# A new order for weight tiles and lead-in in a kernel of retention and two MLPs

## The chip, the cores and the metric

The kernel runs on one core of a Trainium2 chip. The metric is the device time of one execution in microseconds (us). TensorE multiplies matrices, VectorE and ScalarE do elementwise work, GpSimd a little, and SyncE (SP) issues all DMAs from one queue, in order. Each engine works through its own queue in program order and waits on semaphores.

## The reference, cut to what matters

Eight heads of linear attention with a decaying state, then an MLP with a squared ReLU, then RMS norm and a gated MLP. All is float32.

```python
for t in range(S):                                    # B, H, S, D = 4, 8, 768, 64
    state = gamma * state + k[:, :, t] (x) v[:, :, t]  # outer product, per head
    y[:, :, t] = scale * (q[:, :, t] @ state)
x = y as (3072, 512)
h = np.maximum(x @ w_in, 0.0)                         # 512 -> 2048
x = h * h @ w_out                                     # 2048 -> 512
xn = x / sqrt(mean(x * x) + 1e-6) * rms_g
g = xn @ w_gate                                       # 512 -> 1536
out = (g / (1 + exp(-g)) * (xn @ w_val)) @ w_out2
```

## The kernel before, in words

**Retention.** The sequence is cut into 24 chunks of 128 tokens, numbered so that four in a row are the same part of the four batches. For a chunk, `decay_q` and `decay_v` (lines 475 to 490) scale q and v by powers of the decay; `scores` (500) multiplies k and q on TensorE and masks the product on VectorE (line 512); `values` (527) multiplies masked scores and v, and, from chunk 4 on, the old state (`st_in`) and q; `take_x` (546) splits the result into a high part (ScalarE, line 77) and a low part (VectorE, line 74); `into_state` (517) makes the product of k and v, and `take_state` (550) adds it to the state and scales it on ScalarE. `show_state` (492) copies a state to where TensorE reads it.

**Float32 by three products.** TensorE multiplies rounded operands. Each operand is held as high and low part, and `mm3` (151) issues three matmuls: high by high (line 152), high by low (153), low by high (154).

**Weight tiles.** The weights arrive as raw 64-bit words and are put together in steps, one per 128x512 tile, by `tick` (133). In step i, `magnitude` (115) makes the absolute value of tile i+1 from its raw words on ScalarE; `finish1` (91) takes tile i-1, makes its high part on ScalarE (line 94) and hands back a function for the low part on VectorE; `convert` (120) puts tile i together in three VectorE instructions (123 to 127) and fetches tile i+3; the low part comes last. Three buffers `f` hold the tiles in work, and three hold raw words. The first 32 steps are the first MLP's tiles, in and out weight in turn; 36 more are for the second MLP's, which `finish2` (97) writes to DRAM.

**First MLP.** `block1` (635) runs over 16 steps f for each of six blocks of 512 tokens: a projection (`proj`, 12 matmuls), the squared ReLU on ScalarE (`act1`, lines 179 to 182), the low part of s on VectorE, and the output product (`out1`, 12 matmuls) of the step before. `early1` and `late1` (673 to 679) put a weight step ahead of the projection and after it. One retention chunk of the next block is done in each four steps f: scores after the projection of f = 0, 4, 8, 12; state and values one f later; scaling of v and the state copy at f = 2 and of q at f = 3, for the chunk to come. So VectorE's queue has a chunk's q behind the weight steps of that f.

**Lead-in.** Lines 561 to 618 load chunks 0 to 3 and the first weights, run retention for these four, and run the first two weight steps among them. TensorE's sums are in eight banks: `acc` has four, `h` two, `sc` and `xs` one each. A bank is free for the next product when its readers are done. The state products of the four chunks use `sc` and `xs` in turn (line 617).

The order of the work is written out by hand: each engine's queue has the instructions in the order of the program text. The last two thirds of the kernel (second MLP) are not touched.

Of the kernel before, what the change touches and what calls it, by code (L numbers as in the profile page):

```python
# [26 lines left out]
CB = TB // C  # L27
# [18 lines left out]
def retention_then_two_mlps(  # L46
    ctx: ExitStack, tc: tile.TileContext, qT, kT, kn, vn, w1i, w1o, w2g, w2v, w2o, rmsg, tri, qdec, vdec, sdec, out
):
    nc = tc.nc
# [14 lines left out]
    def bank(tag, shape, name, bufs):  # L64
        return ps.tile(shape, F32, tag=tag, name=name, bufs=bufs)
# [10 lines left out]
    def split(dst_h, dst_l, src, el):  # L76
        nc.scalar.copy(dst_h, src)  # L77
        low(el, dst_l, src, dst_h)
# [28 lines left out]
    loads, sizes, done = {}, {}, {}  # L107
    at = [0]
# [6 lines left out]
    def magnitude(i):  # L115
        if i < len(steps):
            sizes[i] = cf.tile([128, 512], F32, tag="f", name="f")
            nc.scalar.activation(sizes[i], loads[i].bitcast(F32)[:, :, 1], AF.Abs, scale=REBIAS)

    def convert(i):  # L120
        raw, f = loads.pop(i), sizes.pop(i)
        m = f.bitcast(I32)
        nc.vector.tensor_scalar(m, m, 3, None, op0=ALU.logical_shift_left)
        nc.vector.scalar_tensor_tensor(
            out=m, in0=raw[:, :, 0], scalar=29, in1=m, op0=ALU.logical_shift_right, op1=ALU.bitwise_or
        )
        nc.vector.scalar_tensor_tensor(
            out=m, in0=raw[:, :, 1], scalar=-(1 << 31), in1=m, op0=ALU.bitwise_and, op1=ALU.bitwise_or
        )
        done[i] = f  # L130
        fetch(i + 3)

    def tick():

        i = at[0]
        if i > len(steps):
            return
        if i == 0:
            magnitude(0)
        magnitude(i + 1)  # L140
        rest_of = None
        if i:
            fn, key, _ = steps[i - 1]
            rest_of = fn(key, done.pop(i - 1))
        if i < len(steps):
            convert(i)
        if rest_of is not None:
            rest_of()
        at[0] = i + 1

# [272 lines left out]
    with tc.manual_schedule():  # L423
        nc.vector.memset(ones, 1.0)

        with ExitStack() as rctx:
# [48 lines left out]
            def decay_q(c, eng):  # L475
                if c < NCH:
                    eng.tensor_tensor(out=chunk[c][0], in0=chunk[c][0], in1=qdec_sb, op=ALU.mult)

            def decay_v(c, eng):

                if c >= NCH:
                    return
                vv = chunk[c][2].rearrange("p a h d -> p (a h) d")
                if eng is nc.scalar:
                    for h in range(H):
                        nc.scalar.activation(vv[:, h, :], vv[:, h, :], AF.Copy, scale=vdec_sb[:, h:h + 1])
                else:
                    eng.tensor_tensor(
                        out=vv, in0=vv, in1=vdec_sb.unsqueeze(2).to_broadcast([128, H, D]), op=ALU.mult
                    )  # L490

            def show_state(c):
                if B <= c < NCH:
                    for b in heads:
                        nc.scalar.copy(st_in[b, :, b], st[c % B][b])
# [4 lines left out]
            def scores(c, tags, early=False):  # L500

                qq, k_, _, _ = chunk[c]
                sc = [bank(*tag) for tag in tags]
                if early:
                    P = wp.tile([128, 2, 512], F32, tag="w", name="Pt").rearrange("p h (a i) -> p h a i", a=NP)
                else:
                    P = rp.tile([128, 2, NP, C], F32, tag="P", name="Pt", bufs=1)
                for p in range(NP):
                    for h, b in enumerate(heads):
                        nc.tensor.matmul(sc[h][:, p, :], k_[b, p, :], qq[b, p, :], start=True, stop=True)  # L510
                for h in range(2):
                    nc.vector.tensor_tensor(
                        out=P[:, h], in0=sc[h], in1=tri_sb.unsqueeze(1).to_broadcast([128, NP, C]), op=ALU.mult
                    )
                pt[c] = P

            def into_state(c, tag, bufs):
                if c // B == CPB - 1:
                    return None
                _, _, vv, kk = chunk[c]  # L520
                kv = bank(tag, [128, NP, D], "kv", bufs)
                for p in range(NP):
                    for h, b in enumerate(heads):
                        nc.tensor.matmul(kv[b, p, :], kk[:, p, h, :], vv[:, p, h, :], start=True, stop=True)
                return kv

            def values(c, tag, bufs):
                P = pt.pop(c)
                qq, _, vv, _ = chunk[c]
                xs = bank(tag, [128, NP, C], "xs", bufs)  # L530

                for p in range(NP):
                    for h, b in enumerate(heads):
                        nc.tensor.matmul(
                            xs[b, p, :], vv[:, p, h, :], P[:, h, p, :], start=(p == 0),
                            stop=(c < B and p == NP - 1), skip_group_check=True,
                        )
                if c >= B:
                    for p in range(NP):
                        nc.tensor.matmul(  # L540
                            xs[:, p, :], st_in[:, p, :], qq[:, p, :], start=False, stop=(p == NP - 1),
                            skip_group_check=True,
                        )
                return xs

            def take_x(c, x, xs):
                o = slice((c % B) * C, (c % B + 1) * C)
                split(x[0][:, :, o], x[1][:, :, o], xs, nc.vector)

            def take_state(c, kv):  # L550
                n = c % B
                if kv is None:
                    return
                if c >= B:
                    nc.vector.tensor_tensor(out=st[n], in0=st[n], in1=kv, op=ALU.add)
                for p in range(NP):
                    nc.scalar.activation(
                        st[n][:, p, :], (st[n] if c >= B else kv)[:, p, :], AF.Copy, scale=sdec_sb[:, p:p + 1]
                    )
# [30 lines left out]

            def decay0(c):
                decay_q(c, nc.vector)
                decay_v(c, nc.scalar)

            decay0(0)
            decay0(1)
            scores(0, early_banks, early=True)
            keep_warm(WARM // 2)
            scores(1, early_banks, early=True)
            decay0(2)  # L600
            xs = values(0, "xs", 1)
            scores(2, early_banks, early=True)
            take_x(0, cur, xs)
            decay0(3)
            xs = values(1, "sc", 1)
            scores(3, early_banks, early=True)
            take_x(1, cur, xs)
            tick()
            xs = values(2, "h", 2)
            take_x(2, cur, xs)  # L610
            tick()
            xs = values(3, "xs", 1)
            take_x(3, cur, xs)
            decay_q(CB, nc.vector)
            decay_v(CB, nc.scalar)
            for c in range(CB):
                take_state(c, into_state(c, "xs" if c % 2 else "sc", 1))
            show_state(CB)

            prev = None  # L620
# [14 lines left out]
            def block1(j, x, ret, early, late):  # L635
                nonlocal prev, at_chunk
                acc = []
                for f in range(NF1):
# [3 lines left out]
                    while ("i", f) not in W:  # L642
                        tick()
# [29 lines left out]
            def early1(f):  # L673
                if at[0] <= n1_steps or f % 2 == 0 or f // 2 < per_block - NF1 // 2:
                    tick()

            def late1(f):
                if at[0] <= n1_steps:
                    tick()

            for j in range(NB - 1):
                nxt = new_x()
                block1(j, cur, nxt, early1, late1)
                cur = nxt
# [11 lines left out]
        xs = prep_x(0, lambda: [quarter[0, h].rearrange("p m n -> p (m n)") for h in range(2)])  # L696
# [48 lines left out]
        for s in range(NS):  # L745
            acc = []
# [14 lines left out]
            xs = iter(())  # L761
            if s + 1 < NS:
                xs = prep_x(
                    2 * (s + 1), lambda: [tp.tile([128, TB], F32, tag="sq", name="yl") for _ in range(2)], lazy=s == 0
                )
# [82 lines left out]
```

## Time and profile before

| | us |
|---|---|
| median of 3 runs | 1208.14 (1207.37 to 1209.44) |
| profiled execution, its own time | 1207.8 |
| its span, first to last instruction | 1206.0 |
| TensorE busy with matmuls | 1174.0 |
| VectorE busy | 706.3 |
| ScalarE busy | 571.4 |

The profile is of one execution. TensorE is shown busy 97% of the span; its matmuls overlap, and their ends are modelled. The first of 40 slices of the span is at six tenths, the next at eight, the rest at nine or more but for the last.

### The profile page before, as it was taken

The page shows a single profiled execution, that of the slowest core. Times are in us where ns is not written, and L with a number is a line of the kernel's source. Part 1 is how long each engine was busy: PE and PEld are TensorE (multiplying, and loading weights), DVE is VectorE, ACT ScalarE, POOL GpSimd, SP SyncE. Part 2 cuts the span into 40 slices and gives each one's busy share as a digit, 9 for nine tenths or more (in the row PEclk, how much of TensorE's full clock was granted, in tenths as well). Part 3 has the DMA queues.
Part 4 walks back from the last instruction along what each step waited for, and adds up shares of the span by engine and source line. Part 5 has one row for each costly group of instructions (what it writes and reads, how often), then busy time and mean ns, then how long its engine had stood idle before and what let it go on. Part 6 is the DMA issues. An engine that isn't in the chain of part 4 may idle for free.

```text
span 1206.0 us, 15522 instructions
## 1 busy us (share of the span) xinstructions
PE 1174.0 (97%) x6006; PEld 952.4 (79%) x6006; DVE 706.3 (59%) x1097; ACT 571.4 (47%) x1084; POOL 95.5 (8%) x76
## 2 busy tenths in 40 slices
PE   6899999999999999999999999999999999999998
PEld 5677788888888887887777788888788888788887
DVE  5788854254344326431654677776677776677740
ACT  6767644444444444333554544544544444444431
POOL 0000031140022104002002000000000000000000
PEclk9999999999999999999999899999999999999999
DMA  8455543442334435311223111133111132111001
GB/s 300 154 186 176 200 140 108 129 149 88 114 116 141 123 94 151 94 36 59 82 79 114 36 36 44 36 105 110 39 35 44 36 123 81 51 35 44 27 1 70
DMA packets 56042, 114.08 MB, mean 95 GB/s; under 512 B 6280, under 2 KB 12576, under 8 KB 55968
## 3 DMA queue, kind: packets, MB, share of 16 engines
q1 hardware_dynamic: 55968, 113.09, 29.7%
q8 instruction: 47, 0.77, 0.3%
q14 instruction: 27, 0.22, 0.1%
HBM read 91.04 MB, written 22.03 MB: 94 GB/s over the span
## 4 chain that ended last, share of the span: by engine, by line
PE 85%; DVE 5%; ACT 5%; issue 2%; DMA 2%; SPq 0%; DVEq 0%; ACTq 0%
PE h L154 7%; PE h L152 6%; PE h L153 6%; PE acc L152 6%; PE acc L153 6%; PE acc L154 6%; PE a L152 5%; PE a L154 5%; PE a L153 5%; PE b L154 4%; PE b L153 4%; PE b L152 4%; PE late L152 3%; PE late L153 3%; PE late L154 3%; PE oacc L154 3%
## 5 line engine op out<-in xcount | busy, mean ns | idle before, releaser
L74 DVE TENSOR_TENSOR s<-r,s 128x512 fp32r<-128x512 f32 x96 | 69.7, 726 | 201.7 <-ACT s L182 201.7
L179 ACT ACTIVATE r<-h 128x512 f32<-128x512 f32 x96 | 57.3, 597 | 224.0 <-PE h L154 224.0
L152 PE MATMUL h<-xh,w_i 128*128 128x512 f32 x384 | 151.9, 395 | 5.6 <-ACT w_i L94 5.6
L152 PE MATMUL acc<-s,w_o 128*128 128x512 f32 x384 | 153.5, 400 | 1.2 <-DVE y L71 1.2
L154 PE MATMUL h<-xh,w_i 128*128 128x512 f32 x384 | 151.6, 395 | 2.1 <-DVE w_i L74 2.1
L153 PE MATMUL acc<-s,w_o 128*128 128x512 f32 x384 | 150.1, 391 | 1.8 <-DVE s L74 1.8
L153 PE MATMUL h<-xl,w_i 128*128 128x512 f32 x384 | 150.3, 391 | 0.0
L154 PE MATMUL acc<-s,w_o 128*128 128x512 f32 x384 | 149.9, 390 | 0.0
L152 PE MATMUL a<-xop,ring 128*128 128x512 f32 x288 | 113.9, 395 | 0.4 <-DVE t L351 0.4
L154 PE MATMUL a<-xop,ring 128*128 128x512 f32 x288 | 112.2, 389 | 0.0
L153 PE MATMUL a<-xop,ring 128*128 128x512 f32 x288 | 112.2, 389 | 0.0
L152 PEld LDWEIGHTS h<-xh,w_i 128*128 128x128 f32 x384 | 72.8, 189 | 24.1 <-ACT w_i L94 8.7
L74 DVE TENSOR_TENSOR ring<-q,ring 128x512 fp32r<-128x512 f32 x90 | 58.8, 686 | 53.3 <-ACT ring L77 53.3
L154 PEld LDWEIGHTS h<-xh,w_i 128*128 128x128 f32 x384 | 72.6, 189 | 21.8 <-DVE w_i L74 6.8
L152 PEld LDWEIGHTS acc<-s,w_o 128*128 128x128 f32 x384 | 72.2, 188 | 17.7 <-DVE y L71 1.6
L153 PEld LDWEIGHTS acc<-s,w_o 128*128 128x128 f32 x384 | 72.2, 188 | 16.8 <-DVE s L74 2.9
L152 PE MATMUL b<-xop,ring 128*128 128x512 f32 x216 | 84.3, 390 | 0.2
L154 PEld LDWEIGHTS acc<-s,w_o 128*128 128x128 f32 x384 | 72.1, 188 | 15.3
L153 PEld LDWEIGHTS h<-xl,w_i 128*128 128x128 f32 x384 | 72.5, 189 | 14.8
L153 PE MATMUL b<-xop,ring 128*128 128x512 f32 x216 | 84.1, 389 | 0.0
L154 PE MATMUL b<-xop,ring 128*128 128x512 f32 x216 | 84.1, 389 | 0.0
L152 PEld LDWEIGHTS a<-xop,ring 128*128 128x128 f32 x288 | 54.2, 188 | 15.5 <-DVE t L351 4.6
(150 smaller groups left out, 2165.1 us busy)
## 6 DMA issues: line engine op xcount, KB each, us to landing
q<-wq SPq DMA_DIRECT2D x72, 256.0 KB, 3.2
raw<-w1i SPq DMA_DIRECT2D x16, 512.0 KB, 3.6
raw<-w1o SPq DMA_DIRECT2D x16, 512.0 KB, 3.6
raw<-w2g SPq DMA_DIRECT2D x12, 512.0 KB, 3.8
raw<-w2v SPq DMA_DIRECT2D x12, 512.0 KB, 3.5
raw<-w2o SPq DMA_DIRECT2D x12, 512.0 KB, 3.9
wq<-f SPq DMA_DIRECT2D x24, 256.0 KB, 3.9
ys<-y SPq DMA_DIRECT2D x24, 256.0 KB, 2.5
```

The lines of the kernel that those rows point to most:

```text
L74: eng.tensor_tensor(out=dst_l, in0=src, in1=dst_h.bitcast(F32), op=ALU.subtract)
L152: nc.tensor.matmul(acc, ah, bh, start=start, stop=False, **more)
L153: nc.tensor.matmul(acc, ah, bl, start=False, stop=False, **more)
L154: nc.tensor.matmul(acc, al, bh, start=False, stop=stop, **more)
L179: nc.scalar.activation(r, h, AF.Relu)
```

## The change

In `tick`, the high part of tile i-1 (`fn`) is issued ahead of the magnitude of tile i+1; with `low_first` the low part is issued ahead of the conversion. In the lead-in, VectorE scales v of chunks 0 to 3 in one instruction each (line 489) where ScalarE did in eight; the first weight step moves ahead of `take_x(1)`, the second behind the state products; values of chunk 3 go to an `h` bank, the four state products to the four `acc` banks, all issued ahead of the second weight step. In the first block an additional step runs where the count of steps reaches 5 and 10, that is at f = 1 and f = 3; the number of steps in all is the same.

```diff
-    def tick():
+    def tick(low_first=False):
...
-        magnitude(i + 1)
-        rest_of = None
+        rest_of = lambda: None
         if i:
             fn, key, _ = steps[i - 1]
-            rest_of = fn(key, done.pop(i - 1))
+            rest_of = fn(key, done.pop(i - 1)) or rest_of
+        magnitude(i + 1)
+        if low_first:
+            rest_of()
         if i < len(steps):
             convert(i)
-        if rest_of is not None:
+        if not low_first:
             rest_of()
...
             def decay0(c):
                 decay_q(c, nc.vector)
-                decay_v(c, nc.scalar)
+                decay_v(c, nc.vector)
...
             scores(3, early_banks, early=True)
+            tick()
             take_x(1, cur, xs)
-            tick()
             xs = values(2, "h", 2)
             take_x(2, cur, xs)
-            tick()
-            xs = values(3, "xs", 1)
+            xs = values(3, "h", 2)
             take_x(3, cur, xs)
+            kvs = [into_state(c, "acc", 4) for c in range(CB)]
+            tick(low_first=True)
             decay_q(CB, nc.vector)
             decay_v(CB, nc.scalar)
             for c in range(CB):
-                take_state(c, into_state(c, "xs" if c % 2 else "sc", 1))
+                take_state(c, kvs[c])
...
             def early1(f):
                 if at[0] <= n1_steps or f % 2 == 0 or f // 2 < per_block - NF1 // 2:
                     tick()
+                    if at[0] in (5, 10):
+                        tick()
```

## Rows read from the trace of the kernel before

**Rows 1.** Stages: us, busy of each engine (x instructions), granted TensorE clock, DMA share.
```profile
36.00:40.00 4.00, 3.32 (x8) 2.69 (x9) 3.90 (x9) 1.19 (x2) 0.00 (x0) 0.57 0.43 131
45.00:150.00 105.00, 100.34 (x549) 76.76 (x548) 87.16 (x149) 75.52 (x161) 0.99 (x1) 1.00 0.57 183
150.00:270.00 120.00, 120.00 (x720) 98.02 (x719) 55.54 (x77) 53.96 (x105) 32.87 (x25) 1.00 0.44 134
```

**Rows 2.** Timeline of TensorE (start, us, operation, idle before): score products in block 1.
```profile
31.76 1.16 PE L510 MATMUL sc<-qnt,kTt 64*128 64x128 f32 x16
61.76 1.16 PE L510 MATMUL sc<-qnt,kTt 64*128 64x128 f32 x16
...
146.25 1.16 PE L510 MATMUL sc<-qnt,kTt 64*128 64x128 f32 x16
172.53 1.16 PE L510 MATMUL sc<-qnt,kTt 64*128 64x128 f32 x16
198.22 1.16 PE L510 MATMUL sc<-qnt,kTt 64*128 64x128 f32 x16
```

**Rows 3.** Waits from 45 to 160: who waited for whom, total, times, longest.
```profile
DVE w_i L74 <- ACT w_i L94: 8.5, 10, 1.1
ACT f L118 <- DVE w_i L74: 7.7, 6, 1.8
```

**Rows 4.** Timeline of VectorE: a weight step in the first block.
```profile
64.16 0.42 DVE L123 TENSOR_SCALAR f<-f 128x512 int32<-128x512 int32 x1
...
65.95 0.68 DVE L74 TENSOR_TENSOR w_i<-f,w_i 128x512 fp32r<-128x512 f32 x1
66.55 0.69 DVE L74 TENSOR_TENSOR s<-r,s 128x512 fp32r<-128x512 f32 x1
```

**Rows 5.** Timeline of ScalarE: the first block.
```profile
48.76 0.60 ACT L179 ACTIVATE r<-h 128x512 f32<-128x512 f32 x1 [0.64 <-PE h L154]
...
61.87 0.60 ACT L179 ACTIVATE r<-h 128x512 f32<-128x512 f32 x1 [1.46 <-PE h L154]
...
63.69 0.66 ACT L118 ACTIVATE f<-raw 128x512 f32<-128x512 f32 x1
64.26 0.60 ACT L94 CAST w_i<-f 128x512 fp32r<-128x512 f32 x1
66.67 0.68 ACT L118 ACTIVATE f<-raw 128x512 f32<-128x512 f32 x1 [1.81 <-DVE w_i L74]
```

**Rows 6.** Timeline of ScalarE: the lead-in.
```profile
9.40 2.02 ACT L486 ACTIVATE stage<-stage,vdec_sb 128x64 f32<-128x64 f32 x8 [1.42 <-DMA stage<-vn]
13.04 2.02 ACT L486 ACTIVATE stage<-stage,vdec_sb 128x64 f32<-128x64 f32 x8 [1.62 <-DMA stage<-vn]
...
23.11 2.01 ACT L486 ACTIVATE vnt<-vnt,vdec_sb 128x64 f32<-128x64 f32 x8
...
26.16 1.84 ACT L557 ACTIVATE st<-kv,sdec_sb 128x64 f32<-128x64 f32 x8 [0.24 <-PE kv L524]
...
29.12 0.82 ACT L495 COPY st_in<-st 64x256 f32<-64x256 f32 x2
```

**Rows 7.** Timeline of VectorE: the lead-in and the first state sum.
```profile
16.16 0.68 DVE L477 TENSOR_TENSOR stage<-stage,qdec_sb 128x512 f32<-128x512 f32 x1
18.11 1.29 DVE L512 TENSOR_TENSOR Pt<-sc,tri_sb 128x512 f32<-128x512 f32 x2 [1.26 <-PE sc L510]
...
45.53 0.41 DVE L555 TENSOR_TENSOR st<-st,kv 128x256 f32<-128x256 f32 x1
```

**Rows 8.** Timeline of TensorE: state products, first and second projection.
```profile
25.43 2.84 PE L524 MATMUL kv<-stage 128*64 128x64 f32 x48 [4.36 <-DVE xl L74]
28.20 0.80 PE L152 MATMUL h<-xh,w_i 128*128 128x512 f32 x1
...
36.68 0.80 PE L154 MATMUL h<-xh,w_i 128*128 128x512 f32 x1 [1.05 <-DVE w_i L74]
```

**Rows 9.** DMA issues of the page: source, count, KB each, us to landing.
```profile
raw<-w1i SPq DMA_DIRECT2D x16, 512.0 KB, 3.6
```

## The prediction

> **What bounds the kernel now.** I read the stage table first. From 45 to 150 us (the first block of the first MLP, where weight tiles are still being made) TensorE shows 100.34 us of matmul in 105 us; from 150 to 270 it shows 120.00 of 120 [rows 1]. So 4.7 us look lost. Then I read the starts of the score products, one group per four steps f, a ruler laid along the program. Without waits the ruler's period is 198.22 - 172.53 = 25.69 us; from 31.76 to 146.25 four periods take 114.49 us, and 4 x 25.69 = 102.76 [rows 2]. So 11.7 us are lost there, 30.00 - 25.69 = 4.3 in the first period and 84.49 - 77.07 = 7.4 in the other three. A short stall costs more than its idle row shows, since the matmuls about it lose their overlap.
>
> The weight-load column bears on this: 76.76 us in 105 against 98.02 in 120 [rows 1]. The Trainium skill ("Perfetto Trace Analysis", Identifying the Most-Contended Engine) says that matmul busy time is a poor measure of headroom and weight-load busy time a good one. By that rule 76.76 / (98.02/120) = 94.0 us of the 105 do work and 11.0 are to be had; by the idle alone 4.7. The trace sides with the rule, and the sum below stands on the ruler alone.
>
> What loses it is a ping-pong. In one weight step ScalarE makes the magnitude of tile i+1, then the high part of tile i-1. The magnitude needs one of three buffers, which VectorE's low part of the step before frees; so ScalarE waits for VectorE (7.7 us in 6 waits), the high part stands behind it, and VectorE waits for the high part (8.5 us in 10) [rows 3]. TensorE gets each tile just too late.
>
> **The change, part by part.** Units: a step of a weight tile on VectorE takes 66.55 - 64.16 = 2.39 us, 1.79 to convert and 0.60 for the low part [rows 4]. On ScalarE the three operations on h take 63.69 - 61.87 = 1.82 us, a magnitude 0.57, a high part 0.60 [rows 5].
>
> *ScalarE's order.* The high part goes ahead of the magnitude. It needs only the conversion of the step before, so the 1.81 us wait at 66.67 [rows 5] no longer holds it; the magnitude still waits, but is needed a full step later. No instruction is added. For the second MLP's tiles the step is a DMA on SP's queue; there the fetch stays behind it, the queue's order is the same, and I put it at nothing: TensorE is at 120.00 of 120 there.
>
> *VectorE scales v.* ScalarE's eight instructions take 2.02 us per chunk [rows 6]; four chunks leave its lead-in. VectorE gets one multiply per chunk. None of this shape on VectorE is in the trace; between the half-wide state sum, 0.41, and the pair of masked products, 1.29, lies the q multiply of the same size, 0.68 [rows 7], and I take that one's step to step, 0.6. The wait moves too: VectorE now stands until v of chunk 1 lands at 9.40 and of chunk 2 at 13.04, where ScalarE stood [rows 6]. Behind the first stand the masks of chunks 0 and 1, some 2.4 us, and q of chunk 2: done by 13.0. Behind the second stands chunk 2's mask, whose scores end at 14.2 (mask to 15.5), and the low part of x(0) (16.1). Then q of chunk 3 runs at about 16.1, as now (16.16). The last v multiply falls into the 1.3 us in which VectorE waits for chunk 3's scores. So the masks at 18.11 [rows 7] stay, and the part costs nothing; if v landed a microsecond later, it would cost that microsecond, up to here.
>
> *State products.* They now wait for the last low part of x (4.36 us), because they share its bank; the first projection follows at 28.20 [rows 8]. In accumulator banks they need only the masks, and run from about 20.4 to 23.2, while VectorE converts. x(1) to x(3) come after the first conversion; the first weight tile's low part lands at 23.5, and the projection starts there, 4.7 us earlier.
>
> *What is late next* is ScalarE. Its queue: conversion 0 follows the masks of chunk 3 (18.11 and some 1.2) and ends at 19.3 + 1.79 = 21.1; first high part and magnitude, to 22.3; then v of chunk 4 with 2.0, four state scalings with 2 x 1.84 = 3.7, the state copy 0.8 [rows 6]: 28.8. High part of the second tile 29.4, magnitude 30.0, operations on h 31.8, high part of the third tile 32.4. VectorE: low part 30.0, masks 31.2, conversion 33.0, low part of the third tile 33.6. The matmul at 36.68 now waits for that low part [rows 8]; it comes at 33.7, 2.9 us earlier, with 0.1 for the signal. The other 1.8 of the 4.7 go into ScalarE's queue.
>
> *More lead.* Two steps are brought forward, to f = 1 and f = 3: 4.8 us of VectorE earlier, none added. Their tiles must be there: a fetch leaves after the conversion three back, lands in 3.6 us [rows 9], and three steps take 7.2. From 33.6 VectorE has low parts of s (0.6), steps 4 to 6, s, x, the state sum (0.4), step 7, conversion 8: 0.6 + 7.17 + 0.6 + 0.6 + 0.4 + 2.39 + 1.79 = 13.55, so 47.15. There it waits: TensorE goes from 36.68 to the operation on the third h at 48.76 in 12.08 us now, so that comes at 45.8, and the high part of step 8 is done at 45.8 + 1.82 + 0.60 = 48.2. Low part, s and conversion 9: 51.2. ScalarE meanwhile makes a magnitude, scales v of chunk 5 (2.0) and copies the state (0.8), so its next high part is done at 52.2; VectorE loses 1.0 again. Low part 52.8, step 10 55.2, step 11 57.6, s 58.2, q of chunk 5 58.8. The next scores need that q: 58.9, against 61.76 now [rows 2], 2.9 us earlier. VectorE sets this point; TensorE is there before, as from 48.76 to 61.87 [rows 5] it takes 13.1 now, some 2 of it stalls, so it could be there at 56.8.
>
> *Then TensorE leads.* VectorE's work per period is 8 x 2.39 + 4 x 0.6 + 1.2 + 0.6 + 0.4 + 0.6 = 24.3 us, under 25.69. With the two waits about v and the state copy, 1.7 to 2.0, it is about 26.1, 0.4 over the ruler; the last period ends its steps early. Gain there 7.4 - 2 x 0.4 = 6.6.
>
> **Sum.** 2.9 + 6.6 = 9.5 us. After 150 us everything only starts earlier. The profiled execution took 1207.8 us, a span of 1206.0 and 1.8 around it; 1198.3 follows. The three runs have a median of 1208.14, 0.3 above it; I write 1198.4.
>
> **Rivals.**
> *VectorE stays the bound* (chance 0.19). It has 24.3 of 25.69 us, and two steps come forward. If its waits per period stay near 3, the period is 27.2, and three of them save 84.49 - 81.6 = 2.9; with the 2.9 of the lead-in 5.8: 1202.3. For it: it is busy 87.16 of 105 us [rows 1]. Against it: the waits are for a high part that now goes first.
> *More than that* (0.10). If the waits at f = 2 and f = 3 vanish, q of chunk 5 is ready at 56.8 and TensorE, by its own pace, too: 4.9 + 7.4 = 12.3 us, 1195.8. Against it: the v scaling and the state copy stay on ScalarE.
> *Slower: the stalls become lumps that lower TensorE's clock* (0.05). Now stalls in the periods are under a microsecond, at full clock; but from 36 to 40, after waits of which the last was 1.05 [rows 8], the clock granted was 0.57 [rows 1], that is mostly its 1.2 GHz level, and 4 us at that cost 1.7. If the wait for q (2.1 us before the scores) came back in each period and brought such a stretch, a period would lose 3.8 instead of the present 2.5 on average; with the scores at 26.0 in the lead-in and 58.9 next, the end would come at 58.9 + 77.1 + 11.4 = 147.4, 1.2 us later than 146.25: 1209.3. It decides from 3.4 lost per period. Against it: the three later q waits shrink as the lead grows. The Trainium skill ("TensorE: Matmul & The Clock Gate", HAM oscillation) has just this rule, that bursts with idle gaps between them run on a lowered clock; by it alone 1209.3 would stand.
> *The lead doesn't build* (0.04): the added steps only take time from VectorE that TensorE gives back as waiting, and only the lead-in gains, some 0 to 3 us: 1206.5.
>
> **How the numbers follow.** My forecast has 0.62. Its own range, from 0.2 to 1.0 lost per later period and the lead-in 1.5 off either way, is 1196 to 1200.5. Reaching to the first two rivals it is 1194.8 to 1203. A gain of 0.2% (2.4 us, about what can be told from no change) is passed by the first three cases and half of the last: faster 0.93, same 0.02, slower 0.05.
>
> **What would show it.** Right: the state products follow the last values without a wait, near 20.4; the first projection near 23.5; a gap of some 5 us before the second; the matmul of 36.68 near 33.7; scores at 58.9, 85, 111 and 136.7; no wait of a projection for a high part after 60 us. Wrong: score starts more than 26.5 apart after 60 us, masks of chunk 3 later than 18.5, the clock below full after 60 us, or anything after 150 us that is not the old trace moved.

## The result, and the profile after

The changed kernel takes 1196.72 us (median of 4 runs, 1195.3 to 1198.1) against 1207.95 (median of 4): a ratio of 0.9905, 95% interval 0.9888 to 0.9922, or 9.4 to 13.5 us less. The prediction was 1198.4, faster by 9.5. The profiled execution took 1198.1, with a span of 1196.3 (before 1206.0), 9.7 less.

Line numbers moved by two: line 510 of before is 512 here, 154 is 156, 179 is 181 (513 and 157 where the old order is put back into the changed kernel). First the stages, with the columns of [rows 1]:

```profile
36.00:40.00 4.00, 4.00 (x42) 3.12 (x41) 3.90 (x8) 3.04 (x6) 0.00 (x0) 0.84 0.61 178
45.00:150.00 105.00, 101.99 (x605) 83.45 (x604) 89.30 (x148) 77.72 (x164) 9.52 (x8) 1.00 0.62 193
150.00:270.00 120.00, 120.00 (x706) 97.46 (x705) 51.97 (x78) 54.07 (x103) 24.01 (x18) 1.00 0.41 126
```

TensorE's matmul time from 45 to 150 rose only from 100.34 to 101.99, its weight-load time from 76.76 to 83.45. By the rule of the Trainium skill that the prediction weighed ("Perfetto Trace Analysis", Identifying the Most-Contended Engine) 83.45 / (97.46/120) = 102.8 of the 105 us now do work, against 94.0 before. The trace agrees with that rule again: matmul time shows 1.7 us of a gain that the weight loads put at 8.8.

The ruler, score products on TensorE's timeline, answers to [rows 2]:

```profile
26.99 1.16 PE L512 MATMUL sc<-qnt,kTt 64*128 64x128 f32 x16
59.33 1.16 PE L512 MATMUL sc<-qnt,kTt 64*128 64x128 f32 x16 [2.26 <-issue]
85.47 1.16 PE L512 MATMUL sc<-qnt,kTt 64*128 64x128 f32 x16 [0.38 <-PE h L156]
111.62 1.16 PE L512 MATMUL sc<-qnt,kTt 64*128 64x128 f32 x16 [0.37 <-PE h L156]
137.33 1.16 PE L512 MATMUL sc<-qnt,kTt 64*128 64x128 f32 x16
```

Against 61.76 and 146.25 of before, 2.43 us are won by the second of these and 8.92 by the last. The periods are 26.14, 26.15 and 25.71. The wait of 2.26 ahead of the scores is that for q, which VectorE begins to scale at 58.55:

```profile
58.55 0.69 DVE L479 TENSOR_TENSOR qnt<-qnt,qdec_sb 128x512 f32<-128x512 f32 x1
```

Waits from 45 to 150, as in [rows 3]:

```profile
ACT w_o L94 <- DVE f L127: 7.3, 4, 2.3
DVE w_o L74 <- ACT w_o L94: 2.7, 3, 1.1
DVE w_i L74 <- ACT w_i L94: 2.4, 5, 0.8
```

ScalarE's magnitudes no longer wait for a low part, and VectorE's waits for the high part of the first weights' tiles fell to 2.4 us (8.5 before, from 45 to 150 as in the longer window of [rows 3]). ScalarE now waits for conversions: it is ahead.

The lead-in on TensorE, answering to [rows 8]: state products, first projection, second projection with its first and third matmul:

```profile
21.04 0.28 PE L526 MATMUL kv<-stage 128*64 128x64 f32 x2
21.15 2.12 PE L526 MATMUL kv<-stage 128*64 128x64 f32 x62
23.40 0.47 PE L154 MATMUL h<-xh,w_i 128*128 128x512 f32 x1
...
32.70 0.79 PE L154 MATMUL h<-xh,w_i 128*128 128x512 f32 x1 [4.55 <-ACT w_i L94]
...
34.13 0.79 PE L156 MATMUL h<-xh,w_i 128*128 128x512 f32 x1 [0.21 <-DVE w_i L74]
```

The first projection moved up by 4.80 us, the matmul that waits for the third tile's low part by 2.55. ScalarE's timeline shows what lies between (states, state copy, then the high parts of the second and third tile):

```profile
25.12 3.35 ACT L559 ACTIVATE st<-kv,sdec_sb 128x64 f32<-128x64 f32 x16
28.26 0.86 ACT L497 COPY st_in<-st 64x256 f32<-64x256 f32 x2
29.14 0.62 ACT L94 CAST w_o<-f 128x512 fp32r<-128x512 f32 x1
...
32.03 0.62 ACT L94 CAST w_i<-f 128x512 fp32r<-128x512 f32 x1
```

And VectorE's: v of chunk 1, scaled once it landed, and the masks of chunk 3 and the low part of the third tile, which follow later:

```profile
10.28 0.69 DVE L490 TENSOR_TENSOR stage<-stage,vdec_sb 128x512 f32<-128x512 f32 x1 [2.02 <-DMA stage<-vn]
...
18.98 1.29 DVE L514 TENSOR_TENSOR Pt<-sc,tri_sb 128x512 f32<-128x512 f32 x2 [0.66 <-PE sc L512]
...
33.39 0.68 DVE L74 TENSOR_TENSOR w_i<-f,w_i 128x512 fp32r<-128x512 f32 x1
```

### The profile page after: what moved, and what is told of

Read it like the earlier page. It is cut to its first block, busy times and chain, and to the rows that moved or that the text cites. A ratio compares the mean times of both kernels' runs of the same rounds, so it can differ in the third digit from the quotient of the medians.

```text
span 1196.3 us, 15490 instructions
## 1 busy us (share of the span) xinstructions
PE 1169.4 (98%) x6006; PEld 953.3 (80%) x6006; DVE 708.8 (59%) x1101; ACT 563.8 (47%) x1052; POOL 94.7 (8%) x76
## 4 chain that ended last, share of the span: by engine, by line
PE 88%; DVE 4%; ACT 3%; DMA 3%; issue 1%; SPq 0%; DVEq 0%; ACTq 0%
PE acc L154 7%; PE acc L155 7%; PE acc L156 7%; PE h L154 7%; PE h L156 7%; PE h L155 7%; PE a L154 5%; PE a L155 5%; PE a L156 5%; PE b L154 4%; PE b L155 4%; PE b L156 4%; PE late L154 3%; PE late L156 3%; PE late L155 3%; PE oacc L156 3%
```

## The experiments

Each kernel was timed in turn with the kernel before on one chip; a ratio is to that. Beside the times stands the ruler: the scores of chunk 5, the three later periods in sum, and the first scores of the second block (its "end"). The later periods tell parts of a microsecond apart where the times scatter by one or two. The lead-in differs from execution to execution: the scores of chunk 4 came at 31.76 to 33.64 in the four profiled executions with the old lead-in, at 26.07 to 27.23 in six with the new one (before, 31.76; change, 26.99). So a microsecond between two kernels in chunk 5 or in the end can be that of the executions; the later periods are the safer comparison.

| kernel | us (runs) | ratio, 95% interval | chunk 5 | 3 periods | end |
|---|---|---|---|---|---|
| before | 1207.95 (4) | 1 | 61.76 | 84.49 | 146.25 |
| order alone | 1206.36 (9) | 0.9975 (0.9966 to 0.9985) | 62.51 | 82.83 | 145.34 |
| lead-in alone | 1203.85 (4) | 0.9959 (0.9944 to 0.9973) | 58.76 | 84.46 | 143.22 |
| two steps alone | 1204.70 (10) | 0.9967 (0.9955 to 0.9979) | 64.50 | 80.91 | 145.41 |
| order, lead-in | 1200.79 (4) | 0.9934 (0.9918 to 0.9949) | 57.36 | 82.82 | 140.18 |
| lead-in, two steps | 1201.05 (4) | 0.9933 (0.9916 to 0.9950) | 61.07 | 79.13 | 140.20 |
| order, two steps | 1201.81 (4) | 0.9942 (0.9927 to 0.9956) | 62.05 | 78.01 | 140.06 |
| all three: the change | 1196.72 (4) | 0.9905 (0.9888 to 0.9922) | 59.33 | 78.00 | 137.33 |
| change, v on ScalarE | 1198.13 (4) | 0.9906 (0.9885 to 0.9926) | 59.67 | 78.02 | 137.69 |
| change, old banks | 1199.26 (4) | 0.9924 (0.9903 to 0.9944) | 61.42 | 77.96 | 139.38 |
| change, q early | 1194.78 (4) | 0.9880 (0.9866 to 0.9895) | 58.03 | 77.43 | 135.46 |
| and states late | 1193.18 (4) | 0.9876 (0.9859 to 0.9892) | 55.76 | 77.44 | 133.20 |
| and low part first | 1192.34 (4) | 0.9865 (0.9841 to 0.9888) | 53.88 | 78.66 | 132.54 |
| change, short copies | 1198.80 (4) | 0.9917 (0.9892 to 0.9941) | 59.40 | 77.97 | 137.37 |

**The new order alone**, on the kernel before:

```diff
-        magnitude(i + 1)
         rest_of = lambda: None
         if i:
             fn, key, _ = steps[i - 1]
             rest_of = fn(key, done.pop(i - 1)) or rest_of
+        magnitude(i + 1)
```

> The kernel before with nothing but the new order inside a weight step (high part ahead of the magnitude). Theory (the order breaks the ping-pong of ScalarE and VectorE): the lead-in stays, score products of chunk 4 within 0.5 us of 31.8; the later periods between score products fall from 28.6 us to 25.9 to 26.5; 1199 to 1202 us. Rival (the lead of two more steps does it, order alone leaves every tile just too late): periods above 27.5, 1204 to 1207 us.

Measured 1206.36 us, periods of 28.06, 28.04 and 26.73. This is nearly all the rival's: order alone takes some 0.55 us off a period that loses 2.9. (The lead-in of this execution ran late, scores of chunk 4 at 32.90, which the theory had within 0.5 of 31.8.) The tile for the next projection is still made while TensorE works on the output product ahead of it. Three timelines show one such place, at f = 6 and 7, ScalarE (the operations on h, then the high part), VectorE (low part), TensorE (the matmul that needs it):

```profile
78.09 0.60 ACT L181 ACTIVATE r<-h 128x512 f32<-128x512 f32 x1 [1.17 <-PE h L156]
...
79.91 0.61 ACT L94 CAST w_i<-f 128x512 fp32r<-128x512 f32 x1
```
```profile
80.55 0.69 DVE L74 TENSOR_TENSOR w_i<-f,w_i 128x512 fp32r<-128x512 f32 x1 [1.66 <-ACT w_i L94]
```
```profile
81.30 0.50 PE L156 MATMUL h<-xh,w_i 128*128 128x512 f32 x1
```

From the first operation on h at 78.09, 3.21 us go by until the low part is multiplied; TensorE has 12 matmuls of an output product to fill them, 2.7 us. The magnitude that used to stand in this chain was 0.57 of it [rows 5]. All that the order gives in this period is won here: counted from the scores, the projection of f = 7 comes 0.5 us earlier than before, that of f = 5 doesn't. The two waits of TensorE in the period stay, 0.36 us at f = 5 and 0.72 at f = 8 (0.35 and 0.74 before):

```profile
87.31 0.50 PE L154 MATMUL h<-xh,w_i 128*128 128x512 f32 x1 [0.72 <-ACT w_i L94]
```

At f = 5 VectorE has its masks and a conversion ahead of the low part, and at f = 8 ScalarE, late from v and the state copy, makes the magnitude ahead of the operations on h instead of behind them.

**Order and lead-in, without the two additional steps:**

```diff
-                    if at[0] in (5, 10):
-                        tick()
```

> The changed kernel without the two additional steps at counts 5 and 10. Theory: with the new order the lead is worth little: the scores of chunk 5 no longer wait for q (start near 57.5 instead of 59.3), projections wait some 0.2 to 0.4 us each for a tile; 1195.5 to 1199 us. Rival (the lead carries the gain): periods above 26.8 us after 60 us, over 1200 us.

1200.79 us; the rival again, and on its number. The scores of chunk 5 come at 57.36, as the theory had it, but the periods are those of order alone (82.82 against 82.83 in sum). So the two steps cost up to 1.97 us by 59.33 and return 4.82 in three periods. Of the 1.97, up to 0.92 can be the execution's: its scores of chunk 4 came at 26.07, those of the changed kernel at 26.99.

**The changed kernel with the old order:**

```diff
         if i:
             fn, key, _ = steps[i - 1]
+        magnitude(i + 1)
+        if i:
             rest_of = fn(key, done.pop(i - 1)) or rest_of
-        magnitude(i + 1)
```

> The changed kernel with the old order inside a weight step (magnitude ahead of the high part), all else as changed. Theory: the ping-pong comes back and eats the lead; VectorE waits again for high parts (over 5 us in all from 45 to 150), periods 26.8 to 28.6 us; 1200 to 1205 us. Rival (with two more steps of lead the order doesn't matter): periods under 26.3 us, 1196 to 1198.5 us.

1201.05 us. The ping-pong is back, as expected, but the lead carries most of it: periods of 26.73, 26.70 and 25.70, just under what the theory said. The waits from 45 to 150 show who waits now:

```profile
ACT f L118 <- DVE w_i L74: 9.5, 6, 2.4
PE sc L513 <- issue: 2.9, 1, 2.9
PE sc L513 <- PE h L157: 1.9, 2, 0.9
```

ScalarE waits with its magnitudes for low parts again, and VectorE comes later to q: the scores wait 2.9, 0.9 and 0.9 us, where they wait 2.26, 0.38 and 0.37 with the new order. That, 2.87 us by the ruler, is what the order is worth beside the lead.

**The changed kernel, v of chunks 0 to 3 scaled by ScalarE:**

```diff
-                decay_v(c, nc.vector)
+                decay_v(c, nc.scalar)
```

> The changed kernel with ScalarE scaling v of chunks 0 to 3, in eight instructions each as before. Theory: this part is worth nothing: masks of chunk 3 within 1 us of the changed kernel's 19.0, first low part of the state's product unmoved, 1195.7 to 1197.7 us. Rival (ScalarE is the next bound, so its 8 us there are a gain): the first high part of a weight tile comes 1.5 us or more later than 22.1, and the time is 1198 to 1200 us.

1198.13 us, ratio 0.9906 where the change has 0.9905. The masks of chunk 3 start at 19.33 (18.98), the first high part at 22.43 (22.09), and the ruler's end is 0.36 us later: in the lead-in and in the time this part of the change is worth nothing that can be measured. But far behind it, as the sixth and last block of the first MLP begins, a wait appears that the changed kernel doesn't have. TensorE's row there, and VectorE's in this kernel and in the changed one, each at the last copy of the fifth block's sums:

```profile
557.76 0.50 PE L154 MATMUL acc<-s,w_o 128*128 128x512 f32 x1 [0.95 <-DVE y L71]
```
```profile
557.01 0.69 DVE L71 COPY y<-acc 128x512 f32<-128x512 f32 x1 [4.40 <-DMA ys<-y]
```
```profile
554.75 0.69 DVE L71 COPY y<-acc 128x512 f32<-128x512 f32 x1 [2.50 <-DMA ys<-y]
```

VectorE waits 4.40 us, not 2.50, for the DMA that stores y, and TensorE 0.95 for VectorE. That is taken up by the experiment with short copies, below.

**The lead-in alone**, the changed kernel with the old order and without the additional steps:

```diff
+        magnitude(i + 1)
+        if i:
             rest_of = fn(key, done.pop(i - 1)) or rest_of
-        magnitude(i + 1)
...
-                    if at[0] in (5, 10):
-                        tick()
```

> The lead-in of the changed kernel alone: old order inside a weight step, no additional steps. Theory (each of the three parts has its own share; the lead-in's is some 2 to 4 us, handed on unchanged): scores of chunk 5 at 57.4 to 58.5 us, the later periods 28 to 28.6 as in the kernel before; 1203 to 1205.5 us. Rival (VectorE is the bound, so what the lead-in wins is lost again as waiting by 60 us): scores of chunk 5 after 60.5 us, 1206 us or more.

1203.85 us, scores of chunk 5 at 58.76, 0.26 behind the theory's range: 3.0 us won by then, and the later periods (84.46) equal those of before (84.49). What the lead-in wins is handed on whole.

**Order and the two steps**, on the kernel before, with its lead-in:

```diff
-        magnitude(i + 1)
         rest_of = lambda: None
         if i:
             fn, key, _ = steps[i - 1]
             rest_of = fn(key, done.pop(i - 1)) or rest_of
+        magnitude(i + 1)
...
+                    if at[0] in (5, 10):
+                        tick()
```

> The kernel before with the new order and the two additional steps, the old lead-in kept. Theory (order and lead only work together, as a tile that is made after the operations on h comes 3.0 us after the projection's end and 2.7 us of cover stand against it): periods after 60 us near 26.1 us, where order alone had 28.0; scores of chunk 5 at 61.5 to 62.5; 1201 to 1203.5 us. Rival (the lead can't build without the earlier lead-in): periods above 27, over 1204 us.

1201.81 us. The periods are those of the changed kernel, 78.01 against 78.00; the lead builds without the earlier lead-in.

**The two steps alone**, on the kernel before:

```diff
+                    if at[0] in (5, 10):
+                        tick()
```

> The kernel before with the two additional steps alone; old order, old lead-in. Theory (lead is what tiles made just in time lack, and it takes off the wait of every projection even in the old order; what is left is VectorE's and ScalarE's ping-pong): periods after 60 us near 26.7 us, as in the changed kernel with the old order; the first block's last scores some 3 us earlier than 146.25; 1204 to 1206 us. Rival (in the old order the steps only take time that TensorE gives back): 1207.5 us or more.

1204.70 us. In the profiled execution the lead-in ran late (scores of chunk 4 at 33.64, before 31.76). Ahead of the scores of chunk 5 TensorE waited 2.85 us for q, and behind them the granted clock fell: 0.51 and 0.64 in these two stretches (columns of [rows 1]), 0.95 from 60 to 95 us.

```profile
66.00:68.00 2.00, 2.00 (x7) 1.52 (x6) 2.00 (x5) 1.97 (x4) 0.00 (x0) 0.51 0.32 57
68.00:70.00 2.00, 2.00 (x7) 1.64 (x6) 1.93 (x4) 0.00 (x1) 0.00 (x0) 0.64 0.84 332
```

From 64.50 the three periods are 28.31, 26.91 and 25.69; the first didn't come as expected, the second did. By an estimate from the two rows the low clock cost 2 x 0.49 + 2 x 0.36 = 1.7 us; without it the first period would be 26.6. The end isn't 3 us earlier in this execution; counted from the scores of chunk 4 (111.77 against 114.49) it is 2.7. The time agrees with the theory.

**The changed kernel with the state products in their old banks and place:**

```diff
-            kvs = [into_state(c, "acc", 4) for c in range(CB)]
             tick(low_first=True)
...
-                take_state(c, kvs[c])
+                take_state(c, into_state(c, "xs" if c % 2 else "sc", 1))
```

> The changed kernel with the four state products back in the sc and xs banks, behind q and v of chunk 4; all else as changed. Theory (ScalarE's queue sets the second projection, so 4 us on the first are worth nothing by themselves): first projection at 26.5 to 27.5 instead of 23.4, scores of chunk 4 near 30 instead of 27, but the second projection within 0.7 us of 32.7 and scores of chunk 5 within 0.7 of 59.3; within 1 us of the changed kernel. Rival (the accumulator banks are the core of the lead-in): scores of chunk 5 after 61 us, 1199 us or more.

1199.26 us, scores of chunk 5 at 61.42: the rival, and my theory of the lead-in's middle fell. TensorE and VectorE of this kernel:

```profile
27.30 0.80 PE L154 MATMUL h<-xh,w_i 128*128 128x512 f32 x1
...
31.18 1.16 PE L512 MATMUL sc<-qnt,kTt 64*128 64x128 f32 x16
...
36.10 0.76 PE L156 MATMUL h<-xh,w_i 128*128 128x512 f32 x1 [1.60 <-DVE w_i L74]
```
```profile
32.37 1.29 DVE L514 TENSOR_TENSOR Pt<-sc,tri_sb 128x512 f32<-128x512 f32 x2 [1.96 <-PE sc L512]
```

The first projection is late by 3.90 us; it follows waits of TensorE and begins on a granted clock of 0.58 (26 to 30 us). The scores of chunk 4 come 4.19 later than in the changed kernel, VectorE's masks wait 1.96 us for them, and the conversion and the third tile's low part stand behind these masks. So the third matmul comes 1.97 later. ScalarE's queue was the bound of the second projection by some two microseconds only (4.19 - 1.97); below it lay this chain through the scores.

**q of the next chunk scaled at f = 2** instead of f = 3 in the first block, on the changed kernel:

```diff
-                    if ret is not None and f % CB == 3:
+                    if ret is not None and f % CB == (3 if j else 2):
                         decay_q(at_chunk + 1, nc.gpsimd if j else nc.vector)
```

> The changed kernel with q of the next chunk scaled at f = 2 of each four instead of f = 3 in the first block, ahead of the two weight steps of f = 3. Theory (VectorE's queue ahead of q sets the scores at 59.3, 85.5 and 111.6): scores of chunk 5 at 56.8 to 57.8, periods 25.7 to 26.2, the wait of the scores for q gone; 1193.5 to 1195.5 us. Rival (the wait only moves to the low part of s or to a tile): scores of chunk 5 above 58.8, 1196 to 1198 us.

1194.78 us. The wait ahead of the scores is gone, as this row of its TensorE timeline shows:

```profile
58.03 1.16 PE L512 MATMUL sc<-qnt,kTt 64*128 64x128 f32 x16
```

That is 0.2 behind the theory's range and 0.8 ahead of the rival's bound; the second projection ran wholly at the lower clock here. The last two periods are 25.70 and 25.69, the ruler's own.

**And the four states behind the weight step that follows the first projection:**

```diff
-            for c in range(CB):
-                take_state(c, kvs[c])
-            show_state(CB)
...
             def late1(f):
                 if at[0] <= n1_steps:
                     tick()
+                if kvs:
+                    keep_states()
```

> As the kernel with q scaled early, and ScalarE scales the four first states and copies one behind the weight step after the first projection instead of ahead of the second tile's high part. Theory (ScalarE's 4.5 us of states hold the second projection back until 32.7, and VectorE's own queue is next, 1.2 us below): the second projection's third matmul near 33.0 instead of 34.1, all later about 1 us earlier; 0.5 to 1.5 us under the kernel with q early. Rival (the states held back now hold the values of chunk 4 or the accumulators): the first output product starts later than 40.5, no gain or a loss of up to 2 us.

1193.18 us. TensorE, the second projection's first and third matmul:

```profile
29.45 0.50 PE L154 MATMUL h<-xh,w_i 128*128 128x512 f32 x1 [2.46 <-ACT w_i L94]
29.79 0.40 PE L155 MATMUL h<-xl,w_i 128*128 128x512 f32 x1
31.68 0.80 PE L156 MATMUL h<-xh,w_i 128*128 128x512 f32 x1 [1.49 <-DVE w_i L74]
```

The high part comes 3.2 us earlier than in the changed kernel, the matmul that waits for the low part 2.45, the scores of chunk 5 2.27 earlier than with q early alone. That is more than the theory said, but the lead-in of this execution was early before the states come into it: the scores of chunk 4 stand at 25.83, against 26.99 in the changed kernel and 27.23 with q early. Without that, some 0.9 us of the 2.27 are left, which is what the theory said. The first matmul still waits for ScalarE, 2.46 us where it waited 4.55; the third now waits 1.49 for VectorE (0.21), whose queue is next, as the theory said.

**And that step's low part ahead of its conversion:**

```diff
-                    tick()
+                    tick(low_first=at[0] == 3)
```

> As the kernel with q early and states late, and the weight step behind the first projection makes its low part ahead of the conversion. Theory (there VectorE's queue, masks and conversion, holds the second projection's third matmul at 31.7): that matmul at 30.0 to 30.5, scores of chunk 5 1.2 to 1.8 us earlier than 55.8; 1190.5 to 1192.5 us. Rival (TensorE's low clock after its waits, or the late state copy, sets the next point): less than 0.5 us gained, 1192.5 to 1194 us.

1192.34 us; scores of chunk 5 at 53.88, 1.88 us earlier, as the theory said (0.08 more than its range). The third matmul is no longer held by VectorE (31.17, later than the 30.0 to 30.5 said, in a lead-in that ran 0.57 later by its scores of chunk 4). But of the 1.88 us only 0.66 are left at the end: the first period is 27.28 us, where it was 26.05, at a new wait:

```profile
53.88 1.16 PE L512 MATMUL sc<-qnt,kTt 64*128 64x128 f32 x16
```
```profile
56.78 0.50 PE L155 MATMUL acc<-s,w_o 128*128 128x512 f32 x1 [1.30 <-DVE s L74]
```

An output product now waits for the low part of s, which stands behind the weight steps in VectorE's queue. This is the fastest version of the study by its median; its interval overlaps with those of the two before it.

**The changed kernel with 32 short copies on ScalarE**, in the block from 150 us on. VectorE's wait for the store of y was 4.3 to 4.6 us in the five traces in which ScalarE scales v (before, order alone, order with two steps, two steps alone, change with v on ScalarE) and 2.5 in the eight others; ScalarE has 1084 instructions in the first kind and 1052 in the changed kernel:

```diff
+            def late1_padded(f):
+                late1(f)
+                for _ in range(2):
+                    nc.scalar.copy(pad, sdec_sb)
...
-                block1(j, cur, nxt, early1, late1)
+                block1(j, cur, nxt, early1, late1_padded if j == 1 else late1)
```

> The changed kernel with 32 short copies added on ScalarE (128x4, into a tile that nothing reads), two for each f in block 1, from 150 us on, where ScalarE is busy for 52 of 120 us. ScalarE then issues as many instructions as where it scales v of chunks 0 to 3 itself; the lead-in is that of the change. Open from the runs so far: VectorE waits 4.3 to 4.6 us for the DMA that wrote y, near 555 to 566 us, in all five traces in which ScalarE scales v, and 2.5 in all eight in which VectorE does. Theory: the number of ScalarE's instructions decides, since an instruction load then falls beside that DMA: a wait of 4.2 to 4.8 us, TensorE held there for 0.8 to 1.2 us, a span 0.8 to 1.4 us above the 1196.3 of the change (32 copies of some 0.2 us lie in ScalarE's idle time), the scores of the second block at 137.3 within 0.4. Rival: the lead-in decides, or chance: 2.5 us, TensorE not held, span 1196.3 within 0.4.

1198.80 us. ScalarE's instructions are 1084 again, and VectorE's row is that of the changed kernel:

```profile
554.79 0.69 DVE L71 COPY y<-acc 128x512 f32<-128x512 f32 x1 [2.50 <-DMA ys<-y]
```

TensorE isn't held. So the number of ScalarE's instructions doesn't decide it: the theory fell. The span is 1197.0, outside of the rival's band by 0.3. The ruler's end is 0.04 later, and the first matmul for the fifth block's norm, at 567.99 us, 0.05 later (567.94 in the changed kernel); the rest lies behind that, where the executions scatter by more.

## Why the prediction was right, and where it wasn't

**The ruler was the right measure.** It set 7.4 us of later periods apart from the lead-in. 6.49 of them came (84.49 to 78.00; 6.6 said), and 2.43 in the lead-in (2.9 said): 8.9 by the ruler, 9.5 said. The span shows 9.7. What is left of it lies behind the ruler, in two parts. Before, TensorE waited 1.18 us at 566.5, and VectorE ahead of it for the store of y, as these rows show (TensorE, then VectorE); the changed kernel has no such wait of TensorE.

```profile
566.54 0.50 PE L152 MATMUL acc<-s,w_o 128*128 128x512 f32 x1 [1.18 <-DVE y L71]
```
```profile
565.80 0.69 DVE L71 COPY y<-acc 128x512 f32<-128x512 f32 x1 [4.63 <-DMA ys<-y]
```

The matmuls for the fifth block's norm, which follow that wait, show what it cost, in the kernel before and in the changed one:

```profile
578.34 0.43 PE L217 MATMUL tot<-sq,ones 128*32 128x128 f32 x8
```
```profile
567.94 0.43 PE L219 MATMUL tot<-sq,ones 128*32 128x128 f32 x8
```

That is 432.09 us behind the ruler's end before and 430.61 now: 1.48 us more. All nine traces without the long wait have 430.6 here, the five with it 431.8 to 432.1. From there to the end the changed kernel took 0.70 longer than before (628.36 against 627.66); this stretch scatters between 626.5 and 629.0 in the fourteen traces, and nothing in the change is known to move it. So 2.43 + 6.49 + 1.48 - 0.70 = 9.7. That it comes to the 9.5 said is in part luck: the ruler gave 0.6 less, and a wait that had no term gave 1.5.

The median's gain, 11.2, is larger than the ruler's; its interval begins at 9.4.

**The lead-in came step by step.** The prediction's numbers stand in brackets. State products at 21.0 (20.4), first projection at 23.4 (23.5), a gap of 4.55 us (some 5), the released matmul at 34.1 (33.7), scores at 59.3, 85.5, 111.6 and 137.3 (58.9, 85, 111, 136.7). From 33 to 37 us TensorE was granted 0.50, the 1.2 GHz level, after its wait of 4.55; before there were two such stretches (26 to 30 and 36 to 40 us, 0.57 each). The sum priced neither. The masks of chunk 3 came at 18.98, not 18.11, which is behind the 18.5 that the prediction named as a sign of being wrong. VectorE took up v of chunk 1 at 10.28, where the prediction had it land at 9.40; but with ScalarE scaling v the masks came at 19.33, so the loads of the execution move this point, and the multiplies need not.

**VectorE's v cost what the q multiply costs**, 0.69 us, and in the lead-in the part was worth nothing, as said and as the kernel with ScalarE doing it shows. What the prediction left out is the wait at 566: in all fourteen traces it goes with the engine that scales v, 1.2 to 1.5 us by the matmuls that follow it. The sum had no term for anything behind the ruler but an earlier start, and named anything else as a sign of being wrong; its size came out right all the same, since 8.9 by the ruler is below the 9.5 said.

**What failed is the share of the new order.** "What loses it is a ping-pong" named the waits that the table of waits shows, and put the gain on the order, with the two steps as lead. Alone the order gave 1.66 of the 6.49 us in later periods, lead-in or not (82.83, 82.82). What loses most is that a tile is made in the last moment, behind the operations on h or behind VectorE's other work: at f = 7 in a chain of 3.2 us against a cover of 2.7. A step more of lead takes the tile out of such chains, and then the order is worth 1.13 of the periods (79.13 against 78.00). The sum was right because both were in it. My expectation for the order alone failed by the same mistake: its time came 4 us above the range.

**What the lead costs** was seen: the wait for q at f = 4, 2.26 us (2.1 said). Scaling q early removed it.

**The rivals.** VectorE did not stay the bound: 89.30 us of 105 busy, and periods of 26.1, where that rival had 27.2. In the changed kernel a lump with a lower clock came once, in the lead-in; the later waits for q were 0.38 and 0.37 and the clock was full from 45 on, through the single wait of 2.26 too. The rule of the Trainium skill ("TensorE: Matmul & The Clock Gate", HAM oscillation) holds for the 4.55 us gap here and didn't reach that wait. The lump that this rival described did come in another kernel: with the two steps alone a wait of 2.85 us for q was followed by 0.51 and 0.64. With the old order in the changed kernel the same wait, 2.85 us at 61.07, left the clock at 1.00 from 61 to 71 us. So a single wait of this length went either way; why isn't shown.

## What to carry to other kernels

Lay a ruler along the program, the starts of one repeated instruction, and take the loss from its stretched periods; the busy share showed a small part of it here (1.7 us of the 8.9 won). Where a producer's last step lies behind a consumer's result, compare the chain's length with the work that covers it, 3.2 against 2.7 us: an instruction taken out of the chain helps by its own length at most, and only where that chain is what the consumer waits for (one place of four here); a step of lead takes out the chain. And when a queue is freed, add up the next one before naming it the bound, through the products it feeds as well.

## What the runs showed of the hardware that was not expected

The wait for the store of y is the first. In the kernel with v on ScalarE an instruction load (queue q8) crosses the DMA engines from 553 to 554 us, while the store of y that VectorE waits for is under way; in the changed kernel it comes from 555 to 556, when VectorE's copy has begun. The DMA queues of these two windows of 1 us, in that order (queue and kind, packets, MB, share of 16 engines):

```profile
q8 instruction: 1, 0.02, 10.2%
```
```profile
q8 instruction: 1, 0.02, 11.7%
```

So it is in all fourteen traces: in the five with the long wait the load lies within it, in the nine others it begins once VectorE's copy has begun. In the kernel with short copies it comes from 555 to 556, as in the changed one, though ScalarE's instructions are as many as before; VectorE's are 1101 in both, and 1097 where ScalarE scales v. The traces do show what the loads of this queue go by: TensorE had started 3121 to 3123 matmuls at the load before this one and 3387 to 3390 at the one behind it, in every kernel; at this one 3250 to 3252 in the five and 3260 to 3264 in the nine. So it is due at about the same point of TensorE's work, and it and the store come in one order or the other. Whether the load, where it comes first, makes the store late, or the store, where it comes first, the load, is not shown, nor what decides between them.

The second: executions with the same lead-in differed by up to 1.9 us in the scores of chunk 4 (31.76, 31.93, 32.90, 33.64 with the old one). VectorE took up q of chunk 2 as it landed, between 11.35 and 12.37 us; in the last of the four, where it came latest, the masks of chunk 3 and what follows are later too. In the last two of the four TensorE's granted clock was 0.50 and 0.56 from 18 to 20 us, where it was 1.00 in the first two; what made it so isn't shown.
